# A convolution and a gated unit in one kernel: seven blocks of the unit's last product move behind the planner's last step, and the output of the last Fourier stage leaves two blocks at a time

## The chip, the cores and the metric

The kernel runs on one core of a Trainium2 chip. A core has five engines with instruction queues of their own: TensorE (PE in the profile, with its weight loads as PEld), VectorE (DVE), ScalarE (ACT), GpSimd (POOL) and SyncE (SP). SP, ACT and POOL can each issue DMAs; 16 DMA engines carry them. The metric is the device time of the program in microseconds; a kernel that is timed several times is given by its median.

## The reference

The input `x` has 2048 tokens of 448 channels in float32. It is normalized per token, and the result `xn` goes two ways, whose sum with `x` is the output:

```python
xn = layernorm(x)
dt = exp(log_dt);  A = -exp(log_A_real) + 1j * A_imag;  C = (C_real + 1j * C_imag) * dt
K  = 2 * real(sum_n C[d, n] * exp(A[d, n] * dt[d] * l))       # 448 kernels of 2048 taps, N = 256 modes
y  = irfft(rfft(xn, 4096) * rfft(K, 4096))[:2048] + xn * D_skip   # a causal convolution per channel
g, u = xn @ w_gate, xn @ w_up                                  # 448 -> 1792
out = x + y + (sigmoid(g) * u) @ w_down                        # 1792 -> 448
```

## The kernel before

**Two programs on one core.** `conv()` builds the convolution: it generates the taps, takes their spectra and those of `xn`, multiplies them and transforms back. `glu()` is the gated unit. Both are Python generators that emit instructions and then yield a cost. A small planner at the end of the kernel always advances the generator whose done share (`done[i] / total[i]`) is the smaller. That sets the order in which the two programs' matmuls stand on PE: a matmul group of one is emitted behind the last group of the other (`issue_after`). `total[1]` is the unit's whole cost less `HELD`, so a smaller `total[1]` makes the unit look further on than it is, and lets the convolution go first more often.

**The gated unit.** The 2048 tokens are 16 blocks of 128, in four accumulators `accs[0..3]` of four blocks each ("acc" in the profile). They are worked in two halves of 8 blocks, and the 14 slices of 128 hidden features in groups of at most three. For a slice and four blocks, `gate` runs two groups of 11 matmuls ("gu", L706; float32 values are split into a high and a low part, so a product is three of them), then ACT takes the tanh (`th`), DVE multiplies (`hf`), ACT casts (`hh`, L722) and DVE takes the rest (`hl`, L724). When a group of slices is through, the down product of each block is 9 matmuls for a group of three slices ("po", L818) and one addition to `acc` on DVE (L823). In the last group of the second half (`final`) the two accumulators are `accs[2]` (blocks 8 to 11) and `accs[3]` (blocks 12 to 15); `t` counts these two, and `b` the blocks in one.

**The last stage of the convolution.** `spectra` goes through 17 steps. A step is `there` ("sp", L902: 32 matmuls into four PSUM banks, copies `kc` on ACT L910, and eight products and sums on DVE L913 to L916) and, one step later, `back` ("pv", L929: 16 matmuls, two copies `vt` on ACT L935). `back` and `there` of a round are emitted together, with the loads of the step three rounds ahead. From `vt` four DMAs on SP store to `v_d` (L947), and when they have landed one DMA on SP loads 16 rows of it back as `vp` (L953). When all steps of a half of the channels (`h`; 224 each) are there, `last(h, m)` for m = 0, 2, 4, 6 runs 32 matmuls each (L964) and adds the result to two blocks in each of two accumulators (L972): m = 0 and 2 to blocks 0 to 7 in `ac`, m = 4 and 6 to blocks 8 to 15 in `accs[2]` and `accs[3]`. The banks of `there`, `back` and `last` are four in turn.

**Order at the end.** At (t, b) = (0, 3) of the final group the unit yields `None`: from there on it is held until the convolution has emitted its last instruction, the `vp` load of the last step. Five blocks, (0, 3) to (1, 3), are thus emitted behind the last `back`, beside the path from `vt` over `v_d` to `vp`. Then `last(1, m)` follows, which needs `vp`.

**The output.** `out` writes four blocks of one half of the channels with four DMAs, 32 partitions each (L238), and deals the DMAs in turn to SP, ACT and POOL. The framework gives the DMAs of SP and ACT together eight completion semaphores in turn and those of POOL eight others; a DMA waits at its queue until the one that had its semaphore before has landed. A block's first channel half is complete when its down products and `last(0, m)` are, its second when `last(1, m)` is.

Of the kernel before, what the change touches and what calls it, by code (L numbers as in the profile page):

```python
# [20 lines left out]
D = 448  # L21
# [12 lines left out]
WP = 5  # L34
WX = 2
HELD = 9
HP = 300
Y0 = (8, 1)
CP = D // 4
H = D // 2  # L40
# [89 lines left out]
def s4d_glu_kernel(ctx, tc, io):  # L130
# [5 lines left out]
    x_t, out_t = tok(io["A_u"][0]), tok(io["out"][0])  # L136
# [90 lines left out]
    accs = [acc_tile() for _ in range(2)]  # L227

    def blocks(t, g, b0, nb):
        return t[g, :, b0 // 8, b0 // 4 % 2, b0 % 4 : b0 % 4 + nb]  # L230

    def out(src, b0, h):

        ds = slice(H * h, H * h + H)
        for g in range(4):
            eng = (nc.sync, nc.scalar, nc.gpsimd)[outs[0] % 3]
            outs[0] += 1
            eng.dma_start(blocks(out_t, g, b0, 4)[:, :, ds], src[32 * g : 32 * g + 32, :, ds])  # L238

    def x_load(dst, b0, nb, engs):  # L240
        for g in range(4):
# [211 lines left out]
    def kgen(pk):  # L453
# [15 lines left out]
        nc.gpsimd.memset(pms[0][:, 6], 1.0)  # L469
        with hp(HP):  # L470
            for _ in powers(pms, 0, None):
# [95 lines left out]

        with hp(HP):
            phase_load(0)
# [8 lines left out]
        for g in range(NCK // NCH):  # L578
            for c in range(NCH):
# [49 lines left out]
                if cn % 4 == 2 and cn > 3 or cn + 1 == NCK:  # L629

                    with hp(HP) if cn + 1 == NCK else tc.issue_after(glu_mm[0].ins):
                        first_stage((cn - 3) // 4 if cn + 1 < NCK else cn // 4)
# [94 lines left out]
    def glu():  # L727
        stores, later = [], []
        for half in range(2):
# [4 lines left out]
            for fs_ in ORDER[half]:  # L734
# [3 lines left out]
                final = half == 1 and fs_ is ORDER[1][-1]  # L738
# [67 lines left out]
                for t in range(2):  # L806
                    acc = accs[2 * half + t]
                    for b in range(4):
                        if final and (t, b) == (0, 3):

                            yield None
                        po = psg.tile([128, D], F32, name="po", tag="gu", bufs=4)
                        bs = slice(128 * b, 128 * b + 128)
                        n = 0
                        with tc.issue_after(sp_mm[0].ins) if glu_on else nullcontext():
                            for (hh, hl), (dh, dl) in zip(hs[t], wts):
                                for a_, w_ in ((hh, dh), (hh, dl), (hl, dh)):
                                    glu_mm[:] = [nc.tensor.matmul(  # L818
                                        po, a_[:, bs], w_, start=(n == 0), stop=(n == 3 * fc - 1)
                                    )]  # L820
                                    n += 1
                        with hp(HP):
                            v.scalar_tensor_tensor(  # L823
                                acc[:, b], po, 0.5, acc[:, b], ALU.mult, ALU.add
                            )
                        yield 0.6 * fc
                        if cross and (t, b) in downs:
                            step(*downs[t, b])
                    if cross:
                        nc.sync.dma_start(acc_d[:, 4 * t : 4 * t + 4], acc)  # L830
                    if final:
                        out(acc, 8 + 4 * t, 0)
                if final:
                    sp_mm[:] = glu_mm
                    for m in range(0, 8, 2):
                        lasts[0](1, m)
                    for t in range(2):
                        out(accs[2 + t], 8 + 4 * t, 1)

    def spectra(pf):  # L840

# [113 lines left out]
        def last(h, m):  # L955

            pos = [bank("pv") for _ in range(2)]
            for i in range(2):
                for g in range(4):
                    for b in range(2):  # L960
                        s = slice(64 * b, 64 * b + 64)
                        w = 8 * g + m + i
                        with after():
                            mm = nc.tensor.matmul(  # L964
                                pos[b][32 * g : 32 * g + 32, i], wf[s, w], vp[h][s, w],
                                start=True, stop=True, skip_group_check=True,
                            )
            sp_mm[:] = [mm]
            for b in range(2):
                q, o, ds = 2 * (m // 4) + b, m % 4, slice(H * h, H * h + H)  # L970
                acc = ac[:, 4 * q + o : 4 * q + o + 2, ds] if q < 2 else accs[q][:, o : o + 2, ds]
                v.tensor_tensor(acc, acc, pos[b], ALU.add)  # L972
            if m % 4 == 2 and m < 4:
                for q in range(2):
                    out(ac[:, 4 * q : 4 * q + 4], 4 * q, h)

        ac = acl[0]
# [11 lines left out]
        for n, (h, k) in enumerate(steps):  # L989
# [21 lines left out]
            while len(wait) > 1 and not (due and wait[0][0] == 1):  # L1011
                t = wait.pop(0)
                turned(*t)
                if t == (0, 28):
                    due = [n + 1]
            prev = (h, k, cur)
            glu_on[:] = [1]
            yield WS
        sp_mm[:] = glu_mm
# [94 lines left out]
    lasts, glu_mm, sp_mm, glu_on, outs, x1s, hfs, xls = [], [], [], [], [0], [0], [], []  # L1114
    xq, psc, raws, acl, marks, slots, pqs = list(x_first), [], [], [], [None, None], {}, []
    W1s, GGs, act = [], [], []
    gens = [conv(), glu()]
    total = [sum(Y0) + 11 * WP + 8 * WX + 14 + NCK * WK + HOLE + 17 * WS, 2 * (4 + NFT * 14.8) - HELD]
    done = [0.0, 0.0]
# [40 lines left out]
```

## Time and profile before

| | |
|---|---|
| median of 3 runs | 730.58 us (728.54 to 733.38) |
| profiled execution | 727.83 us, of which the profile's span is 726.1 us |
| PE busy | 677.6 us, 93% of the span |
| DVE busy | 565.7 us, 78% |
| ACT busy | 420.6 us, 58% |
| POOL busy | 384.2 us, 53% |
| DMA | 115.71 MB, mean 159 GB/s |
| granted TensorE clock, mean | 0.98 |

The profile is one execution. Times in its rows are microseconds from the start of the span. A row of the timeline gives start, duration, engine, line, operation, output and inputs, a count of merged instructions and, in brackets, how long the engine had been idle and what ended that. The chain of waits is followed back from the last instruction: each piece was released by the one before it. A "q" behind an engine is its instruction queue, where DMAs are issued.

### The profile page before, as it was taken

Reading aid. Unit: us, or ns where it says so; the run is one execution under the profiler, and the core shown is the slowest. Engines: PE = TensorE matmul, PEld = TensorE weight load, DVE = VectorE, ACT = ScalarE, POOL = GpSimd, SP = SyncE. Lnnn points to the kernel's source line nnn. Section 1 sums busy time; section 2 is a strip of 40 time slices with the busy share of each in tenths; the row PEclk is TensorE's granted clock in tenths of the full one; section 3 lists DMA queues with packets and bytes.
Section 4 is the critical chain, followed back from the end, with each engine's and each line's share of the span. In section 5 each row is a group of like instructions: output and inputs, shape, how many; then the busy total and the mean of one; then the engine's idle time right before and its main releaser. Section 6 shows DMA issues by size and latency. Waiting matters only on the chain.

```text
span 726.1 us, 19068 instructions
## 1 busy us (share of the span) xinstructions
PE 677.6 (93%) x7780; PEld 533.8 (74%) x7780; DVE 565.7 (78%) x776; ACT 420.6 (58%) x650; POOL 384.2 (53%) x423
## 2 busy tenths in 40 slices
PE   2898799899998999998999999999999999999994
PEld 1674688787886888655778887888877787767783
DVE  5699997699999999999499988986956555664553
ACT  3645455578787788898388678767643312323310
POOL 2110018698899988788557856767844002431001
PEclk9998899999999999999999999999999999999998
DMA  9946328525414554454952232232269999999646
GB/s 203 229 108 183 104 80 248 164 93 177 167 51 135 185 158 147 135 162 130 270 183 102 83 108 97 71 108 94 58 172 271 273 235 234 233 244 221 166 131 162
DMA packets 92710, 115.71 MB, mean 159 GB/s; under 512 B 12112, under 2 KB 81104, under 8 KB 92368
## 3 DMA queue, kind: packets, MB, share of 16 engines
q1 hardware_dynamic: 83312, 94.03, 47.2%
q10 hardware_dynamic: 6736, 14.57, 6.4%
q0 software_dynamic: 2576, 5.90, 3.3%
q8 instruction: 61, 1.00, 0.6%
q14 instruction: 25, 0.20, 0.1%
HBM read 69.70 MB, written 44.76 MB: 158 GB/s over the span
## 4 chain that ended last, share of the span: by engine, by line
PE 58%; DVE 17%; POOL 8%; DMA 7%; issue 3%; ACT 3%; SPq 2%; ACTq 0%; POOLq 0%; DVEq 0%
PE gu L706 23%; PE po L818 12%; PE sp L902 7%; PE ko L614 5%; PE pv L929 4%; POOL me L511 4%; PE tr L533 3%; DVE Et L599 2%; DVE Et L598 2%; DVE Ft L600 2%; DVE hl L724 2%; POOL mf L511 2%; DMA acc_d<-acc 1%; DVE wl L761 1%; DVE pm L447 1%
## 5 line engine op out<-in xcount | busy, mean ns | idle before, releaser
L511 POOL TENSOR_TENSOR me<-me,pm 128x32 f32<-128x32 f32 (+1 forms) x168 | 155.9, 928 | 78.1 <-DVE Et L599 65.5
L511 POOL TENSOR_TENSOR mf<-mf,pm 128x64 f32<-128x64 f32 (+1 forms) x112 | 116.5, 1040 | 4.9
L706 PE MATMUL gu<-xh,wh 128*128 128x512 f32 x336 | 101.1, 407 | 2.5 <-ACT xh L219 2.5
L706 PE MATMUL gu<-xh,wl 128*128 128x512 f32 x336 | 95.4, 392 | 0.0
L706 PE MATMUL gu<-xl,wh 128*128 128x512 f32 x336 | 95.1, 390 | 0.0
L818 PE MATMUL po<-dh,hh 128*128 128x448 f32 x224 | 86.8, 387 | 6.0 <-DVE acc L823 2.5
L598 DVE TENSOR_TENSOR Et<-me,S 128x1024 f32<-128x1024 f32 x56 | 81.8, 1460 | 7.2 <-ACT S L544 5.5
L599 DVE TENSOR_TENSOR Et<-me,S 128x1024 f32<-128x1024 f32 x56 | 79.3, 1415 | 7.8 <-ACT me L524 7.7
L818 PE MATMUL po<-dl,hh 128*128 128x448 f32 x224 | 84.5, 377 | 0.0
L541 ACT ACTIVATE S<-tr 128x1024 f32<-128x1024 f32 x56 | 57.8, 1032 | 45.3 <-PE tr L533 40.3
L600 DVE TENSOR_TENSOR Ft<-mf,S 128x1024 f32<-128x1024 f32 x56 | 78.7, 1405 | 6.8 <-ACT S L544 5.0
L818 PE MATMUL po<-dh,hl 128*128 128x448 f32 x224 | 83.7, 375 | 0.0
L706 PEld LDWEIGHTS gu<-xh,wh 128*128 128x128 f32 x336 | 62.3, 193 | 21.3 <-ACT xh L219 4.0
L722 ACT CAST hh<-hf 128x512 fp32r<-128x512 f32 x56 | 35.0, 625 | 70.0 <-DVE hf L717 57.6
L706 PEld LDWEIGHTS gu<-xh,wl 128*128 128x128 f32 x336 | 62.9, 188 | 14.9 <-DVE pl L307 0.7
L706 PEld LDWEIGHTS gu<-xl,wh 128*128 128x128 f32 x336 | 63.0, 188 | 13.9 <-issue 0.7
L614 PEld LDWEIGHTS ko<-Et,Ft 128*32 128x32 f32 x3584 | 53.8, 110 | 25.7 <-issue 14.7
L614 PE MATMUL ko<-Et,Ft 128*32 128x64 f32 x3584 | 63.9, 222 | 7.6 <-DVE Ft L600 4.2
L717 DVE SCALAR_TENSOR_TENSOR hf<-th,gu 128x512 f32<-128x512 f32 x56 | 38.2, 682 | 38.4 <-PE gu L706 28.0
L544 ACT ACTIVATE S<-S,hpi 128x1024 f32<-128x1024 f32 x56 | 65.7, 1173 | 0.0
L823 DVE SCALAR_TENSOR_TENSOR acc<-po,acc 128x448 f32<-128x448 f32 x80 | 48.5, 616 | 21.7 <-PE po L818 21.7
L724 DVE TENSOR_TENSOR hl<-hf,hh 128x512 fp32r<-128x512 f32 x56 | 51.2, 915 | 13.2 <-ACT hh L722 13.2
(196 smaller groups left out, 1286.5 us busy)
## 6 DMA issues: line engine op xcount, KB each, us to landing
sk_d<-sk ACTq DMA_DIRECT2D x14, 512.0 KB
sx<-x_d SPq DMA_DIRECT2D x32, 224.0 KB
skl<-sk_d SPq DMA_DIRECT2D x16, 448.0 KB
vp<-v_d SPq DMA_DIRECT2D x16, 448.0 KB
v_d<-vt SPq DMA_DIRECT2D x62, 112.0 KB
wt_d<-wh SPq DMA_DIRECT2D x9, 512.0 KB
wt_d<-wl SPq DMA_DIRECT2D x9, 512.0 KB
wl<-wt_d SPq DMA_DIRECT2D x9, 512.0 KB
```

The lines of the kernel that those rows point to most:

```text
L511: ins = nc.gpsimd.tensor_tensor(m[:, :, w + a : 2 * w : n], m[:, :, a:w:n], par(base + i).unsqueeze(2).to_broadcast([128, 4 * DC, w // n]) ...
L541: nc.scalar.activation(rows(cs), pv, AF.Abs)
L544: sins[:] = [nc.scalar.activation(cs, cs, AF.Sin, scale=-TWO_PI, bias=hpi)]
L598: v.tensor_tensor(Et[:, :, :, 32:64], two(me[:, :, 32:64]), S[:, 1::-1], ALU.mult)
L599: v.tensor_tensor(Et[:, :, :, 0:32], two(me[:, :, 0:32]), S[:, 1:3, :, ::-1], ALU.mult)
L600: fts[:] = [v.tensor_tensor(Ft, two(mf), S[:, 3:5], ALU.mult)]
L614: nc.tensor.matmul(ko[32 * j : 32 * j + 32, sl], Ft[:, cc, DC * h + 4 * q + j], Et[:, cc, DC * h + 4 * q + j], start=(k == 0), stop=(k == ...
L706: glu_mm[:] = [nc.tensor.matmul(ps, a_, b_, start=(n == 0), stop=(n == len(mm) - 1))]
L724: v.tensor_tensor(hl, hf, hh, ALU.subtract)
L818: glu_mm[:] = [nc.tensor.matmul(po, a_[:, bs], w_, start=(n == 0), stop=(n == 3 * fc - 1))]
L823: v.scalar_tensor_tensor(acc[:, b], po, 0.5, acc[:, b], ALU.mult, ALU.add)
L902: mm = nc.tensor.matmul(to, tb[:kk, t, 64 * c : 64 * c + 64], rhs, start=True, stop=True, skip_group_check=True,)
```

## The change

Four things change.

- The unit is held from (0, 1) on, not from (0, 3): seven blocks are kept for the time behind the last `back`.
- Of these, five ((0, 1) to (1, 1)) are emitted ahead of `last(1, m)` as before, and two ((1, 2) and (1, 3)) behind it. Each of the two leaves at once with both channel halves, by four DMAs. The first halves of blocks 8 to 11 leave behind (0, 3), those of blocks 12 and 13 behind (1, 1).
- `last(1, m)` hands out its two blocks per accumulator at once, where it had waited for four: eight DMAs at m = 0 and at m = 2, four (of `accs[2]`) at m = 4 and at m = 6. The second halves of blocks 12 and 13 follow behind m = 6.
- `LATE = 3.6` is taken from `total[1]` after round 11 of `spectra`, so that the planner's order shifts from there.

```diff
+LATE = 3.6
...
-    def out(src, b0, h):
-
-        ds = slice(H * h, H * h + H)
+    def out(src, b0, h=None):
+
+        ds = slice(0, D) if h is None else slice(H * h, H * h + H)
         for g in range(4):
             eng = (nc.sync, nc.scalar, nc.gpsimd)[outs[0] % 3]
             outs[0] += 1
-            eng.dma_start(blocks(out_t, g, b0, 4)[:, :, ds], src[32 * g : 32 * g + 32, :, ds])
+            eng.dma_start(blocks(out_t, g, b0, src.shape[1])[:, :, ds], src[32 * g : 32 * g + 32, :, ds])
...
-                        if final and (t, b) == (0, 3):
+                        if final and (t, b) == (0, 1):
 
                             yield None
...
+                        if final and t == 1 and b > 1:
+                            out(acc[:, b : b + 1], 12 + b)
+                        if final and (t, b) == (1, 1):
+                            out(acc[:, 0:2], 12, 0)
+                            sp_mm[:] = glu_mm
+                            for m in range(0, 8, 2):
+                                lasts[0](1, m)
+                            out(acc[:, 0:2], 12, 1)
                         yield 0.6 * fc
                         if cross and (t, b) in downs:
                             step(*downs[t, b])
                     if cross:
                         nc.sync.dma_start(acc_d[:, 4 * t : 4 * t + 4], acc)
-                    if final:
-                        out(acc, 8 + 4 * t, 0)
-                if final:
-                    sp_mm[:] = glu_mm
-                    for m in range(0, 8, 2):
-                        lasts[0](1, m)
-                    for t in range(2):
-                        out(accs[2 + t], 8 + 4 * t, 1)
+                    if final and t == 0:
+                        out(acc, 8, 0)
...
-            if m % 4 == 2 and m < 4:
+            if h == 1 and m < 4:
+                for q in range(2):
+                    out(ac[:, 4 * q + m : 4 * q + m + 2], 4 * q + m, h)
+            elif h == 1:
+                out(accs[2][:, m - 4 : m - 2], 4 + m, h)
+            elif m == 2:
                 for q in range(2):
                     out(ac[:, 4 * q : 4 * q + 4], 4 * q, h)
...
             prev = (h, k, cur)
+            if n == 11:
+                total[1] -= LATE
             glu_on[:] = [1]
```

Up to `last(0, 0)` and `last(0, 2)`, the first of the L964 rows below, PE's order is what it was. On PE just behind them, before the change ("gu" is half a `gate`, the five rows from `xh,wh` to `xl,wh`; "pv" with `yy,bk` is `back`):

```order
L964 MATMUL pv<-vp,wf 32x224 x32
L706 MATMUL gu<-xh,wh 128x512 x3
L706 MATMUL gu<-xr,wh 128x512
L706 MATMUL gu<-xh,wl 128x512 x3
L706 MATMUL gu<-xr,wl 128x512
L706 MATMUL gu<-xl,wh 128x512 x3
L706 MATMUL gu<-xh,wh 128x512 x3
L706 MATMUL gu<-xr,wh 128x512
L706 MATMUL gu<-xh,wl 128x512 x3
L706 MATMUL gu<-xr,wl 128x512
L706 MATMUL gu<-xl,wh 128x512 x3
L929 MATMUL pv<-yy,bk 128x224 x8
```

And in the same place with the change, where every line number is one or three higher:

```order
L967 MATMUL pv<-vp,wf 32x224 x32
L707 MATMUL gu<-xh,wh 128x512 x3
L707 MATMUL gu<-xr,wh 128x512
L707 MATMUL gu<-xh,wl 128x512 x3
L707 MATMUL gu<-xr,wl 128x512
L707 MATMUL gu<-xl,wh 128x512 x3
L932 MATMUL pv<-yy,bk 128x224 x8
L905 MATMUL sp<-skl,tb 64x224 x4
L905 MATMUL sp<-sx,tb 64x224 x4
L905 MATMUL sp<-skl,tb 64x224 x4
L905 MATMUL sp<-sx,tb 64x224 x4
L967 MATMUL pv<-vp,wf 32x224 x32
```

Round 12 (`back`, `there` and `last(0, 4)`, `last(0, 6)`) stands half a `gate` earlier, and so it goes on. Counted from these rows, the halves of `gate` that stand ahead of the six remaining `back`s were 2, 4, 5, 7, 7 and 7 and are 1, 2, 4, 5, 7 and 7; of the final group's blocks of "po", one and three stood ahead of the last two `back`s, and now none and one.

At PE's end, before the change (the last block, `last(1, m)`, the end):

```order
L818 MATMUL po<-dh,hh 128x448
L818 MATMUL po<-dl,hh 128x448
L818 MATMUL po<-dh,hl 128x448
L964 MATMUL pv<-vp,wf 32x224 x64
L1156 UNCONDITIONAL_BRANCH
```

And with the change, where the first three rows below `last(1, m)` stand six times, for blocks (1, 2) and (1, 3):

```order
L967 MATMUL pv<-vp,wf 32x224 x64
L819 MATMUL po<-dh,hh 128x448
L819 MATMUL po<-dl,hh 128x448
L819 MATMUL po<-dh,hl 128x448
```

Eighteen matmuls of "po" have gone from ahead of the last stage to behind it. The queue of SP at its end, before the change:

```order
L947 DMA v_d<-vt 32x4x224 x4
L238 DMA out_dram<-acc 32x4x224
L953 DMA vp<-v_d 16x7168
L238 DMA out_dram<-acc 32x4x224 x2
L238 DMA out_dram<-ac 32x4x224 x2
L238 DMA out_dram<-acc 32x4x224 x3
```

And with the change:

```order
L950 DMA v_d<-vt 32x4x224 x4
L956 DMA vp<-v_d 16x7168
L239 DMA out_dram<-acc 32x4x224
L239 DMA out_dram<-acc 32x2x224 x2
L239 DMA out_dram<-ac 32x2x224 x5
L239 DMA out_dram<-acc 32x2x224 x4
L239 DMA out_dram<-acc 32x448 x3
```

The `vp` load stands ahead of the first output DMA, and behind it SP issues 15 outputs in place of 8. In the same stretch ACT issues 14 and POOL 15, each in place of 8.

## The prediction

> **What bounds the kernel now.** First the page, by engines and by slices of 18.2 us:
>
> ```profile
> span 726.1 us, 19068 instructions
> ...
> PE 677.6 (93%) x7780; PEld 533.8 (74%) x7780; DVE 565.7 (78%) x776; ACT 420.6 (58%) x650; POOL 384.2 (53%) x423
> ...
> PE   2898799899998999998999999999999999999994
> ```
>
> PE is the bound, and in the second half almost without a gap. All that the change moves lies in the last four or five slices. So I look there next, at what PE waits for from 640 us on:
>
> ```profile
> PE pv L964 <- DVE pd L914: 1.2, 1, 1.2
> PE pv L964 <- DMA vp<-v_d: 1.0, 1, 1.0
> ```
>
> These are two waits, 2.2 us in all, both ahead of a `last`. The first lies ahead of the place where the order begins to differ and stays as it is. Everything else up to the last `last` is PE's own time: a matmul taken from ahead of it moves the end forward, as long as no chain of waits turns up in its place. The chain of waits over the end, start and duration:
>
> ```profile
> 690.08 2.02 PE po L818 x9
> 692.10 1.71 PE pv L929 x16
> 693.81 3.18 PE sp L902 x32
> 696.99 3.85 PE po L818 x18
> 700.84 1.76 PE pv L929 x16
> ...
> 705.00 2.83 DMA v_d<-vt
> ...
> 707.91 4.82 DMA vp<-v_d
> ```
>
> The last `back` starts at 700.84, behind three blocks. From there the path goes over the memory to `vp`, beside which PE works on five blocks. Behind that, PE's last row, DVE's and the end of the queues:
>
> ```profile
> 712.86 4.30 PE L964 MATMUL pv<-vp,wf 64*32 64x224 f32 x128 [1.00 <-DMA vp<-v_d]
> ...
> 711.89 0.62 DVE L823 SCALAR_TENSOR_TENSOR acc<-po,acc 128x448 f32<-128x448 f32 x1 [1.20 <-PE po L818]
> 713.92 2.21 DVE L972 TENSOR_TENSOR ac<-ac,pv 128x448 f32<-128x448 f32 x4 [1.41 <-PE pv L964]
> 716.06 2.21 DVE L972 TENSOR_TENSOR acc<-acc,pv 128x448 f32<-128x448 f32 x4
> ...
> L1156 POOLq DRAIN  x3: 46/102/6607, 718.6 to 725.7; - x3
> L1156 SPq DRAIN  x3: 7/7/7, 724.6 to 725.4; - x3
> ...
> 717.00:718.00 1.00, 0.15 (x4) 0.00 (x0) 1.00 (x3) 0.00 (x0) 0.54 (x1) 1.00 0.85 242
> 722.00:723.00 1.00, 0.00 (x0) 0.00 (x0) 0.00 (x0) 0.00 (x0) 0.00 (x0) 0.50 1.03 323
> 723.00:724.00 1.00, 0.00 (x0) 0.00 (x0) 0.00 (x0) 0.00 (x0) 0.00 (x0) 0.50 0.35 117
> ```
>
> The last two numbers of a window's row are the busy share of the DMA engines and GB/s. From 717 to 723 us the DMA engines are full, at 242 to 323 GB/s, with the second channel halves of all 16 blocks (1.84 MB; at some 285 GB/s 6.4 us). SP, which waits for every DMA, is through at 724.6. POOL's drain, which begins with its last DMA at 718.6 and is the 6.6 us one of the three, ends at 725.2, 0.6 us later; then come 0.9 us. So the tail behind the start of `last` at 712.86 is 11.7 us to SP and 12.3 us to POOL.
>
> **The change part by part.** I count from 712.86, the start of the last `last`, and then its tail.
>
> *Two blocks leave the path.* The piece at 696.99 is 18 matmuls, 3.85 us. They now stand behind `last`; one block remains ahead of the last `back`. Does the `back` then wait for its inputs? DVE needs until about 2.3 us after the last "sp" for them, and the first `back` matmuls need only the first half of them. At 690.08 one block, 2.02 us, already stood between the two, and "pv" followed at 692.10 with no gap. So: **-3.85 us**.
>
> *The planner's shift.* Round 12 comes half a `gate` earlier: one half (2.7 us) lies between `last(0, 2)` and its `back`, not two. What PE, ACT and DVE did there:
>
> ```profile
> 649.49 5.21 PE gu L706 x22
> 654.70 1.71 PE pv L929 x16
> 656.42 3.18 PE sp L902 x32
> 659.60 2.65 PE pv L964 x64
> ...
> 650.62 3.87 ACTq L238 DMA_DIRECT2D out_dram<-ac  x3
> 654.53 0.62 ACT L722 CAST hh<-hf 128x512 fp32r<-128x512 f32 x1 [8.94 <-DMA out_dram<-ac]
> ...
> 656.45 0.97 ACT L935 COPY vt<-pv 128x448 f32<-128x448 f32 x2 [0.80 <-PE pv L929]
> ...
> 658.20 0.62 DVE L913 TENSOR_TENSOR yy<-kc,sp 128x448 f32<-128x448 f32 x1 [2.33 <-PE sp L902]
> 658.74 0.61 DVE L914 TENSOR_TENSOR pd<-kc,sp 128x448 f32<-128x448 f32 x1
> ```
>
> ACT stands in its three output issues until 654.5, and behind them in its queue are the cast `hh` and then `vt`, whose banks `there` needs. Before, the 5.21 us of "gu" covered that. Now `back` runs from 652.2 to 653.9, `there` would end at 657.1 and `last` follow at once. But `vt` can only be copied after 654.53 + 0.62 = 655.15, and ends at 656.1; the second pair of banks of `there`, wanted at 655.5, comes 0.2 to 0.6 us late. `kc` stands behind `vt`: the first product pair of DVE then runs from 656.65 to 657.75, where `last` wants its bank at 657.3 (0.5 us), and the second half of `last` loses some 0.3 us likewise. I take **+1.1 us**, between 0 (all of it taken up) and 2.2 (each doubled). The DMAs of the round (four stores, four loads, three `vp`) go 1 to 4 us earlier on SP, which stood idle there from 652.6 to 657.0; later rounds have one or two halves of `gate` between "sp" and "pv" as before and cost nothing.
>
> *The gap of the last stage.* It holds five blocks as before, but the outputs of blocks 8 to 11 leave behind the third block of the five, not the first, some 3.6 us later against `back`. How long SP waited between its last store and `vp`, in the last round but one and in the last:
>
> ```profile
> 694.40 3.17 SPq L947 DMA_DIRECT2D v_d<-vt  x4
> 699.12 0.53 SPq L953 DMA_DIRECT2D vp<-v_d  x1
> 703.14 2.46 SPq L947 DMA_DIRECT2D v_d<-vt  x4
> 705.65 0.59 SPq L238 DMA_DIRECT2D out_dram<-acc  x1
> 707.91 0.53 SPq L953 DMA_DIRECT2D vp<-v_d  x1
> ```
>
> 699.12 - 697.57 is 1.55 us; 707.91 - 705.60 is 2.31 us, with the outputs beside the stores. Without them `vp` starts 0.75 us earlier, and its 4.82 us still cover the wait of 1.00 us. I take **-0.7 us**, between -1.0 (the wait is all there is to win) and +0.5 (the outputs now lie beside the landing of `vp`).
>
> Sum: `last` starts at 712.86 - 3.85 + 1.1 - 0.7 = 709.4.
>
> *The tail.* `last` lasts 4.30 us and the two blocks 3.85 us; then the addition of 0.62 us. The last block is ready 8.8 us behind 709.4, and its second DMA on SP is issued some 0.45 us later. Rows of L238, the outputs around 650 us (few others beside them) and the ones from 712 us on (full engines):
>
> ```profile
> DMA to landing us min/median/max: 2.4/2.5/2.6
> ...
> DMA to landing us min/median/max: 3.2/4.4/4.8
> ```
>
> Meanwhile the other 1.6 MB begins to leave with m = 0, 1.7 us behind the start (713.92 + 0.62 against 712.86), 1.1 us sooner than before (half of the 2.21 us). Allowing 1.8 us until the engines are full, with 5.6 us at some 285 GB/s it is through about 9.1 us behind the start. So the last block finds the engines nearly empty and I take 2.5 us: landed at 11.75, against 11.7 before, **0**; between -0.3 and +1.9 (4.4 us).
>
> *POOL's drain.* Its last DMA comes at 8.8 behind `last` now, and came at 5.7 (718.6). What the drain of 6.6 us waits for, one execution doesn't tell. If it is as long whenever it begins, it ends at 709.4 + 8.8 + 6.6 = 724.8 against 725.2: the kernel ends **0.4 us** earlier and nearly all of the win is lost. If it follows the landing of POOL's own DMAs (718.58 + 4.4 = 723.0, and 2.2 us more), it ends at 718.2 + 2.8 + 2.2 = 723.2: **-2.0 us**. If it follows the last landing of all, **-3.4 us**. I take the middle one: POOL's is the queue that the drain stands in.
>
> Sum: 727.83 - 2.0 = 725.8 us in terms of the profiled execution. The median of the runs stands 2.75 us above that execution, so in its terms 730.58 - 2.0 = **728.6 us**. A change of this kernel below 1%, 7.3 us, can't be told from none.
>
> **The rivals.** *The drain has a fixed length.* For it: it begins with the last DMA, and SP was through 0.6 us before it ended. Against: 6.6 us is far more than the other two drains, 0.05 and 0.1 us. 727.4 in the profile's terms, 730.2 by the median.
>
> *The whole win.* The drain ends with the landings: 727.83 - 3.4 = 724.4, by the median 727.2.
>
> *Slower: small output DMAs that wait for each other.* In place of 16 outputs of 115 KB behind `last` there are 28 of 57 KB and eight for the last two blocks. SP and ACT have 24 of these and eight completion semaphores, so three go through each, one after the other. If a DMA of half the size takes as long to land under load (4.4 us), the third lands at 1.7 + 3 x 4.4 = 14.9 us behind `last`, where 11.7 was: +3.2 us; with the upper stall of 2.2 us the sum is -3.85 + 2.2 - 0.7 + 3.2 = **+0.9 us**, 731.5 by the median. It decides once a landing takes more than (11.7 - 1.7) / 3 = 3.3 us. Against it: 4.4 us is the time in full engines, half of the bytes in flight empty sooner, and behind the queued outputs on SP, ACT and POOL stands nothing but outputs. The Trainium skill ("DMA: Bandwidth & Descriptors", section on bandwidth) speaks for this rival: it would have DMAs batched, and counts transfers under 64 KB as bound by their descriptors, with 138 GB/s at 64 KB. By that rate, an estimate, 1.84 MB would take 13.3 us in place of 6.4. The trace disagrees as far as it goes: DMAs of 115 KB, many in flight, ran at up to 323 GB/s, close to what that page has for 1 MB (341). No run shows 57 KB.
>
> **How the numbers follow.** The middle drain 0.40, the fixed one 0.25, the whole win 0.20, the slower rival 0.15. No case reaches 7.3 us on its own; only with the scatter of the runs (728.54 to 733.38) could it: faster by over 1% 0.05, slower 0.07, within 0.88. The range: below, 727.2 and a scatter of 1.8; above, the slower rival's 731.5 with 0.7 on top: 725.4 to 732.2.
>
> **What would show it.** In the profile after: the last L964 starts near 709.4, with a wait for `vp` under 0.5 us; two new short waits of PE at "sp" and L964 near 655 to 661 us; 18 "po" behind L964; the last landing some 11.7 us behind its start; POOL's drain then tells which of the three it is. I am wrong if PE waits more than 2.2 us near round 12, if `vp` lands later against `back` than it did, or if the output queues are still at work 3 us after the last addition has been issued.

## The result and the profile after

The changed kernel took **728.32 us** (median, 725.02 to 736.09) beside 731.47 us of the kernel before on the same chip (728.20 to 738.99): a ratio of **0.9952, 95% interval 0.9930 to 0.9974**, some 3.5 us faster. The ratio leaves out the one run of 736.09 us, which fell into a slower state. The forecast was 728.6 us and "within 1%" (7.3 us). The profiled execution took 725.02 us against 727.83, 2.8 us less. Repeated among other kernels, the changed kernel came to 728.24 beside 730.35, ratio 0.9988 (0.9962 to 1.0013; the two medians alone stand at 0.9971): the gain is small enough that a second set of runs doesn't separate it from none. What speaks for a gain all the same is the whole of the runs below: all nine sets with the two blocks behind `last` came out between 0.9940 and 0.9988, the two without at 0.9999 and 1.0008.

The page of the changed kernel, by engines and PE's slices:

```profile
span 723.2 us, 19101 instructions
...
PE 676.3 (94%) x7780; PEld 532.4 (74%) x7780; DVE 565.1 (78%) x776; ACT 420.8 (58%) x650; POOL 384.5 (53%) x430
...
PE   2998799997998999998999999999999999999996
```

PE does the same 7780 matmuls; its last slice is fuller (6 tenths, 4 before), since the two moved blocks stand in it. The chain that ended last, from behind the last `there` on, start and duration:

```profile
694.67 2.02 PE po L819 x9
696.69 1.71 PE pv L932 x16
698.40 9.49 PE po L819 x45
707.89 1.67 PE pv L967 x64
709.58 2.55 PE pv L967 x64
712.13 2.06 PE po L819 x9
714.21 0.64 DVE acc L824
714.85 0.28 issue
715.13 0.47 POOL out_dram L239
715.63 0.51 POOL out_dram L239
716.14 0.82 issue
716.97 0.52 POOLq L1166
```

One block stands ahead of the last `back`, five behind it, and the chain goes straight from the five to `last`: the step over the memory (`v_d`, `vp`), which was on it before, is gone. Behind `last` come two blocks, and then not DVE or a landing but POOL's queue. PE's row in the timeline, with no releaser in brackets behind the last `last`, and the two waits near the first one:

```profile
647.63 0.96 PE L967 MATMUL pv<-vp,wf 64*32 64x224 f32 x16 [0.41 <-DVE pd L917]
...
658.27 0.96 PE L967 MATMUL pv<-vp,wf 64*32 64x224 f32 x16 [0.40 <-DVE pd L917]
...
707.82 4.30 PE L967 MATMUL pv<-vp,wf 64*32 64x224 f32 x128
```

The last `last` starts at **707.82** (712.86 before, 709.4 forecast). What follows it took 15.41 us to the end of the span; before, 13.20. So of 5.04 us won up to there, 2.2 were lost behind it. The queue rows of the end (kind, number, and durations in ns: least, median, most), to be read beside those of the kernel before in the prediction:

```profile
L1166 POOLq DRAIN  x3: 46/93/5495, 717.0 to 723.0; - x3
L1166 SPq DRAIN  x3: 7/7/7, 721.0 to 722.7; - x3
```

POOL's drain begins at 717.0 and takes 5.5 us, to 722.5; SP was through at 721.0. Before, it took 6.6 us, from 718.6 to 725.2, with SP through at 724.6.

### The profile page after: what moved, and what is told of

It is laid out like the page before. It is cut to its first block, busy times and chain, and to the rows that moved or that the text cites. A ratio compares the mean times of both kernels' runs of the same rounds, so it can differ in the third digit from the quotient of the medians.

```text
span 723.2 us, 19101 instructions
## 1 busy us (share of the span) xinstructions
PE 676.3 (94%) x7780; PEld 532.4 (74%) x7780; DVE 565.1 (78%) x776; ACT 420.8 (58%) x650; POOL 384.5 (53%) x430
## 4 chain that ended last, share of the span: by engine, by line
PE 62%; DVE 16%; ACT 8%; DMA 7%; issue 4%; SPq 2%; POOL 1%; ACTq 0%; DVEq 0%; POOLq 0%
PE gu L707 24%; PE po L819 15%; PE sp L905 7%; PE ko L615 6%; PE pv L932 4%; PE tr L534 3%; DVE Et L600 2%; DVE Ft L601 2%; DVE Et L599 2%; DVE hl L725 1%; DMA acc_d<-acc 1%; DVE pm L448 1%; ACT S L545 1%; DMA xe<-in_A_u_dram 1%; DVE wl L762 1%
## 5 line engine op out<-in xcount | busy, mean ns | idle before, releaser
L512 POOL TENSOR_TENSOR me<-me,pm 128x32 f32<-128x32 f32 (+1 forms) x168 | 146.1, 870 | 83.5 <-DVE Et L600 70.8
L512 POOL TENSOR_TENSOR mf<-mf,pm 128x64 f32<-128x64 f32 (+1 forms) x112 | 120.7, 1078 | 4.9
L615 PE MATMUL ko<-Et,Ft 128*32 128x64 f32 x3584 | 65.5, 225 | 8.1 <-DVE Et L599 4.6
L725 DVE TENSOR_TENSOR hl<-hf,hh 128x512 fp32r<-128x512 f32 x56 | 51.8, 925 | 12.5 <-ACT hh L723 12.5
```

The lines of the kernel that those rows point to most:

```text
L512: ins = nc.gpsimd.tensor_tensor(m[:, :, w + a : 2 * w : n], m[:, :, a:w:n], par(base + i).unsqueeze(2).to_broadcast([128, 4 * DC, w // n]) ...
L615: nc.tensor.matmul(ko[32 * j : 32 * j + 32, sl], Ft[:, cc, DC * h + 4 * q + j], Et[:, cc, DC * h + 4 * q + j], start=(k == 0), stop=(k == ...
L725: v.tensor_tensor(hl, hf, hh, ALU.subtract)
```

## The experiments

To compare executions I cut each profile at two points: the start of the first `last(0, 0)` and that of the last stage's `last(1, 0)`, called L from here on. "First" is the time by which PE is late at the first `last` (over its undisturbed 2.65 us) and by which the `gate` behind it is slow; "round 12" is what `there` and `last` of that round take over 3.18 and 2.65 us; "to L" goes from the first point to the second, "end" from L to the end of the span, "drain" is when POOL's drain ends behind L. All in us, from one profile each; before and after are the first two rows. The ratio is that to the kernel before, with its 95% interval.

| kernel | first | round 12 | to L | drain | end | ratio |
|---|---|---|---|---|---|---|
| before | 1.12 | 0 | 67.20 | 12.31 | 13.20 | 1 |
| after | 0.36 | 0.36 | 62.31 | 14.64 | 15.41 | 0.9952 (0.9930 to 0.9974) |
| the shift alone | 0 | 2.31 | 67.86 | 12.16 | 13.04 | 0.9999 (0.9966 to 1.0031) |
| without the shift | 0 | 1.38 | 64.07 | 14.56 | 15.34 | 0.9983 (0.9952 to 1.0013) |
| outputs by four | 4.81 | 0 | 66.59 | 14.30 | 15.08 | 0.9983 (0.9951 to 1.0014) |
| last two blocks not on POOL | 2.67 | 0 | 64.35 | 11.51 | 13.59 | 0.9955 (0.9920 to 0.9991) |
| both of these | 5.36 | 0 | 67.06 | 11.67 | 13.33 | 0.9960 (0.9931 to 0.9989) |
| no late output on POOL | 0 | 0 | 61.61 | 6.70 | 15.04 | 0.9972 (0.9945 to 1.0000) |
| outputs by two alone | 2.94 | 0 | 68.81 | 12.89 | 13.67 | 1.0008 (0.9969 to 1.0048) |
| after, again | 0.76 | 1.72 | 64.17 | 14.57 | 15.35 | 0.9988 (0.9962 to 1.0013) |
| no late output on POOL, drain late | 0 | 0 | 61.59 | 13.45 | 15.09 | (one execution) |
| `wh`, `wl` in pieces | 0.81 | 1.42 | 63.81 | 14.58 | 15.36 | 0.9966 (0.9933 to 0.9998) |
| by four, last two not on POOL, in pieces | 0 | 1.02 | 62.67 | 11.83 | 13.48 | **0.9940 (0.9914 to 0.9967)** |

The columns add up. In all nine profiles that have the whole order of the changed kernel, "to L" less "first" and "round 12" is 61.6 to 61.8. Of the kernel before (67.20 - 1.12) it is 66.1, and in the other profile with that order, "outputs by two alone", 65.9. So the change of order is worth **some 4.4 us** (4.1 to 4.5 by the choice of profiles), and the two columns ahead are what an execution adds to it, up to 5.4 us. That is why medians, not single spans, are compared, and why a tail is read from L on.

**The shift alone.** The kernel before with the planner's table alone; no block moves behind `last`:

```diff
+LATE = 3.6
+            if n == 11:
+                total[1] -= LATE
```

> The planner's shift alone (LATE in the kernel before; the unit is held from (0, 3), outputs as before). The order then has one block ahead of the last back and seven beside the path to vp. My account: PE's work ahead of the last stage is as before; the seven blocks cover the wait for vp (1.0 us goes), a stall of some 0.4 us comes at round 12 as in the changed kernel. The last stage starts 0.3 to 1.0 us earlier than before and the span ends as much earlier: 725.1 to 725.8 us against 726.1. Rival, that the shift is what won the time and not the two blocks: the last stage starts 3 to 5 us earlier and the span is near 723.

It took 730.49 us beside 731.22: no difference. Its waits of PE, summed, number and longest:

```profile
PE sp L903 <- ACT vt L936: 1.4, 1, 1.4
PE pv L965 <- DVE pd L915: 0.7, 1, 0.7
```

Seven blocks then lie behind the last `back`, and the wait for `vp` of 1.00 us is gone, but round 12 pays 2.1 us in waits, where 0.4 had been expected. Without that, "to L" is 65.6 us, 0.5 less than before and within what was expected; with it, the shift by itself wins nothing.

**Without the shift.** The changed kernel with `LATE = 0.0`:

> The changed kernel with LATE = 0. The last there is then followed directly by the last back, with no block between. My account: PE waits for DVE's products there, 1.5 to 2.3 us, the 0.4 us stall at round 12 goes; the last stage starts 1 to 2 us later than in the changed kernel (at 709 to 710 us) and the span is 724.3 to 725.2. Rival, that the shift does nothing: 723.2 as in the changed kernel and no wait of PE at that back above 0.5 us.

It took 729.80 us beside 731.22. Its waits of PE:

```profile
PE pv L932 <- DVE yy L918: 0.9, 2, 0.7
PE sp L905 <- ACT vt L938: 0.7, 1, 0.7
PE pv L967 <- DVE pd L917: 0.6, 1, 0.6
```

The last `back` stands directly behind the last `there` and waits 0.9 us for `yy` (1.5 to 2.3 expected), which the one block ahead of it hides in the changed kernel. That is the worth of the shift for the two moved blocks. And round 12 stalls here too, against what was expected, so the stall isn't the shift's alone. ACT's rows there, of this kernel and of the second profile of the changed one:

```profile
654.49 4.22 ACTq L239 DMA_DIRECT2D out_dram<-ac  x3
658.75 0.62 ACT L723 CAST hh<-hf 128x512 fp32r<-128x512 f32 x1 [10.44 <-DMA out_dram<-ac]
...
659.76 0.95 ACT L938 COPY vt<-pv 128x448 f32<-128x448 f32 x2
```

```profile
653.13 3.76 ACTq L239 DMA_DIRECT2D out_dram<-ac  x3
656.94 0.62 ACT L723 CAST hh<-hf 128x512 fp32r<-128x512 f32 x1 [9.53 <-DMA out_dram<-ac]
657.46 0.96 ACT L938 COPY vt<-pv 128x448 f32<-128x448 f32 x2
```

The three output issues hold ACT's queue for about 4 us, and `hh` and `vt` come straight behind. What PE made of that in the second profile:

```profile
656.12 0.93 PE L905 MATMUL sp<-sx,tb 128*64 128x224 f32 x8
658.04 0.98 PE L905 MATMUL sp<-skl,tb 128*64 128x224 f32 x8 [0.99 <-ACT vt L938]
...
661.98 0.96 PE L967 MATMUL pv<-vp,wf 64*32 64x224 f32 x16 [0.56 <-DVE pd L917]
```

How late the round is follows from one time. In all ten profiles with the shift, what round 12 pays is, to within 0.1 us, how far the end of ACT's third output issue trails the start of `back`, less 1.6 us, and nothing below that: 1.93 us behind and 0.36 paid in the changed kernel, 3.30 and 1.72 in its second profile, 1.52 and 0 in "no late output on POOL, drain late". Each time this third issue left within 0.04 us of the landing of the DMA that had its semaphore before. This is read from the profiles; no run set that time by itself.

**Outputs by four.** The changed kernel, but behind `last(1, m)` blocks 0 to 11 leave by four blocks (12 DMAs of 115 KB), not by two (24 of 57 KB):

```diff
-            if h == 1 and m < 4:
-                for q in range(2):
-                    out(ac[:, 4 * q + m : 4 * q + m + 2], 4 * q + m, h)
-            elif h == 1:
-                out(accs[2][:, m - 4 : m - 2], 4 + m, h)
-            elif m == 2:
+            if m == 2:
                 for q in range(2):
                     out(ac[:, 4 * q : 4 * q + 4], 4 * q, h)
+            elif h == 1 and m == 6:
+                out(accs[2][:, 0:4], 8, h)
```

> The changed kernel, but the second halves of blocks 0 to 11 leave by four blocks again (eight DMAs behind m = 2 and four behind m = 6, not eight, eight, four and four). Theory that the eight semaphores of SP and ACT hold back the last block's DMAs: with 12 DMAs less, the last block's four are issued within 1.0 us of its addition (they took until 2.4 us behind it), the last landing is 11.4 to 12.0 us behind the start of the last stage in place of 12.8, and the span is 0.5 to 1.3 us shorter, 722 to 722.7. Rival, that the early start of the output pays more: the engines are still full when the last block comes, the last landing is 12.8 us or more behind, and the span is 723.2 to 724.5.

The last output was issued at L + 10.1 in place of 11.25, so the small DMAs did wait for each other; but it landed at 12.5 in place of 12.8, and POOL's drain still ended last: the end moved by 0.3 us, to L + 15.1. The landing was expected at 11.4 to 12.0 by the one account and at 12.8 or later by the other, so it bears out neither.

**The last two blocks not on POOL.** The changed kernel, its two whole blocks dealt to SP and ACT alone:

```diff
-            eng = (nc.sync, nc.scalar, nc.gpsimd)[outs[0] % 3]
+            eng = (nc.sync, nc.scalar)[outs[0] % 2] if h is None else (nc.sync, nc.scalar, nc.gpsimd)[outs[0] % 3]
```

> The changed kernel, but blocks 14 and 15 leave by SP and ACT alone, so that POOL's last DMA is issued near 714 us and not 717. What does POOL's drain wait for? If it lasts 5.5 to 6.6 us from POOL's last DMA, or ends 2.2 to 2.8 us behind the landing of POOL's own DMAs, it ends near 720.5, ahead of SP, and SP's drain (721 to 722) sets the end: span 722.3 to 723.0. If it waits for the last landing of all queues (+1.8 us as in the changed kernel), it still ends last, near 722.5 to 723.5, and the span is 723.2 to 724.2.

The queue rows of its end:

```profile
L1166 POOLq DRAIN  x3: 46/93/5372, 717.8 to 725.0; - x3
L1166 SPq DRAIN  x3: 7/7/7, 724.4 to 724.7; - x3
```

POOL's drain ran from 717.8 to 723.1, SP was through at 724.4: POOL no longer sets the end. Against L (711.63) the end comes at 13.6 in place of 15.4, 1.8 us sooner. The medians don't show that gain: the ratio is 0.9955 beside 0.9952. The drain ended 1.1 us ahead of the last landing of all (L + 12.6), so it doesn't wait for that.

**Both.** Outputs by four, and the last two blocks on SP and ACT:

> Outputs behind `last` by four blocks (12 DMAs of 115 KB over the three engines), and the last two blocks on SP and ACT alone. Theory: two things sit one behind the other in the tail of the changed kernel, POOL's drain (2.2 to 2.8 us behind the landing of POOL's own last DMA) and, right under it, output DMAs of SP and ACT that wait for a completion semaphore. With both eased POOL's last DMA goes out near +6.2 us behind the start of the last `last`, lands near +8.9, its drain ends near +11.5; the last output is issued near +10.0 (not +11.25) and lands near +12.1; the kernel ends near +12.9 instead of +15.4, 2.5 us sooner than the changed kernel, a median ratio to the kernel before of about 0.992. Rival: the landing is set by the bytes in the engines, not by the semaphores; then it lands at +12.6 as with the last two blocks off POOL alone, and ends at +13.6.

The end is at L + 13.3, 2.1 us sooner than in the changed kernel. It lies between the two accounts (12.9 with the semaphores, 13.6 with the bytes in the engines), so how much of the landing is due to which stays open. The median, 727.75 beside 730.35, shows little of it: this profile, and perhaps other executions too, lost 5.4 us at the first `last`, on which below.

**No late output on POOL.** Outputs by two as in the changed kernel, but all that come behind the start of `last(1, 0)` on SP and ACT (`if h != 0` in the line above):

> Outputs by two blocks as in the changed kernel, but all 36 output DMAs behind the start of the last `last` on SP and ACT, none on POOL. Theory (semaphores): those two engines share eight completion semaphores, so 4 to 5 DMAs go through each in turn in place of 3; POOL's drain is off the path, but the last output is issued 1.5 to 2.5 us later than the +11.25 of the changed kernel, lands near +15 and the kernel ends near +15.5, no sooner than the changed kernel. Rival (the drain alone sets the end, the wait for semaphores is harmless): the last landing stays at +12.6 and the end is at +13.6, 1.8 us sooner than the changed kernel.

The last output was issued at L + 12.4 (11.25 in the changed kernel), landed at 14.1, and the end is at 15.0: with all late outputs on two queues hardly anything is won, though the last issue came 1.1 us later and not 1.5 to 2.5. SP's rows of the outputs:

```profile
709.92 5.26 SPq L239 DMA_DIRECT2D out_dram<-ac  x8
715.40 4.92 SPq L239 DMA_DIRECT2D out_dram<-acc  x10
```

The issues themselves, counting one long one of 1.9 us, fill 8.4 of these 10.4 us; ACT's fill 8.4 of 11.1. Between them lie 2.0 and 2.7 us, less than the 3.3 and 4.5 us that lie between twelve issues each in the changed kernel, and a landing took 1.9 us at the median where it had taken 2.7. So this run doesn't show that the wait for completion semaphores grows with the number of DMAs: here it is mostly the number of issues on two queues. POOL's queue row:

```profile
L1166 POOLq DRAIN  x3: 46/93/5707, 709.2 to 723.0; - x3
```

The drain took its 5.7 us here as well, far from the end and for nothing.

**The drain by itself.** The same kernel with one cast on POOL behind the last addition, whose result nothing uses. POOL's DMAs have all landed then:

```diff
+                        if final and (t, b) == (1, 3):
+                            nc.gpsimd.tensor_copy(d_low(), acc[:, b])
```

> The kernel with all late output DMAs on SP and ACT, and one cast of 0.6 us on POOL behind the last addition (its result is used nowhere), so that POOL's drain begins near +9.6 behind the start of the last `last`, some 5 us after POOL's own last DMA has landed (near +4.7). If the drain follows the landings of POOL's own DMAs alone, nothing is left to wait for: it ends less than 1 us after it began, near +10.5, and SP sets the end near +15.0. If it has a floor of its own of 5.2 to 5.7 us, as the lengths of ten profiles (5.2 to 6.6) would also allow, it ends near +15.0 and the kernel near +15.8. If it waits for the last landing of all (near +14), it ends near +14.5 to +16.

The timeline row of the cast, and the queue row:

```profile
716.85 0.56 POOL L830 CAST dl<-acc 128x448 fp32r<-128x448 f32 x1 [7.31 <-DVE acc L824]
```

```profile
L1168 POOLq DRAIN  x3: 46/102/4593, 716.8 to 722.8; - x3
```

POOL's last DMA had landed at 712.8, 4 us earlier, and still the drain took 4.6 us (4.0 behind the end of the cast). So waiting for its own landings can't be all that the drain does: a part of 4 to 4.6 us is its own. None of the three ends expected (near +10.5, +15.0, +14.5 to 16) is the one measured, +13.45, and it is one execution; whether a drain behind a cast is as long as one behind nothing at all no run shows. Waiting for every landing is excluded again (it ended 0.7 us ahead of the last one).

**Outputs by two alone.** The kernel before, with only the outputs behind `last(1, m)` by two blocks:

```diff
-            if m % 4 == 2 and m < 4:
+            if h == 1:
+                for q in range(2) if m < 4 else (2, 3):
+                    src = ac[:, 4 * q + m : 4 * q + m + 2] if q < 2 else accs[q][:, m - 4 : m - 2]
+                    out(src, 4 * q + m % 4, h)
+            elif m == 2:
                 for q in range(2):
                     out(ac[:, 4 * q : 4 * q + 4], 4 * q, h)
```

> The kernel before with one part of the change alone: behind `last(1, m)` the outputs leave by two blocks, no block of the gated unit is moved. Theory: the first bytes leave 1.1 us sooner, the last addition still ends at +5.4 behind the start of the last `last`, and the DMAs of half the size wait through the semaphores; the two cancel within 0.7 us, landing +10.8 to +11.8, POOL's own last landing +9.5 to +10.5, end +12.5 to +13.6 (before: +13.2); ratio 1.000 within 0.003. Rival (the slower rival of the prediction): three DMAs go one after the other through a semaphore, the last one lands at +14.9, the kernel is 3 us slower, ratio 1.004. Other rival: outputs by two are a gain of their own of 1 us or more, end below +12.2.

Landing at L + 11.1 (11.5 before), end at 13.7 (13.2, and 13.6 at most expected): the two effects of smaller DMAs cancel, a little on the wrong side, because POOL issues 11 of them at 0.54 us each behind L where it had issued 5, so that its drain begins 1.5 us later and ends 0.6 us later. Ratio 1.0008. This part of the change is worth nothing by itself.

**The changed kernel again.**

> The changed kernel itself, beside the others on the same chip. Theory: its end lies 15.4 us behind the start of the last `last`, of which POOL's drain ends 2.2 to 2.8 us behind the landing of POOL's own last DMA; the wait of PE in round 12 is between 0 and 1.3 us, with the wait at the first `last` ahead of it; a ratio of 0.995 within 0.003. Rival: the first measurement was a lucky one and the ratio is 1.000.

Tail and drain are as in its first profile (15.35 and 14.57 behind L), round 12 stalled 1.7 us (1.3 at most expected), and the ratio was 0.9988, just outside the 0.992 to 0.998 expected. Its interval and the first one overlap (0.9962 to 0.9974), so the first may have been on the lucky side; 1.000 isn't excluded by this set alone.

**POOL's `wh` and `wl` in pieces.** The profile of "both" lost most at the first `last`. DVE's and POOL's rows around it:

```profile
645.83 0.61 DVE L917 TENSOR_TENSOR pd<-kc,sp 128x448 f32<-128x448 f32 x1
646.36 1.16 DVE L918 TENSOR_TENSOR yy<-yy 128x224 f32<-128x224 f32 x1
647.55 2.42 DVE L919 TENSOR_TENSOR yy<-pd 128x224 f32<-128x224 f32 x1
```

```profile
646.23 1.04 POOL L769 CAST wh<-wraw 128x1024 fp32r<-128x1024 f32 x1 [5.63 <-DMA wraw<-in_B_w_up_dram]
647.36 2.37 POOL L770 TENSOR_TENSOR wl<-wraw,wh 128x1024 fp32r<-128x1024 f32 x1
```

A `yy` takes 0.38 to 0.39 us alone. Here the first lasts until POOL's cast ends (647.3), the second until `wl` ends (649.7). `pd` is late by that, and PE waited for it:

```profile
PE pv L967 <- DVE pd L917: 2.8, 1, 2.8
```

Products with one operand in PSUM (`sp`) aren't held. POOL's and DVE's rows of the changed kernel in its first profile:

```profile
643.39 2.36 POOL L770 TENSOR_TENSOR wl<-wraw,wh 128x1024 fp32r<-128x1024 f32 x1
```

```profile
644.18 0.62 DVE L916 TENSOR_TENSOR yy<-kc,sp 128x448 f32<-128x448 f32 x1 [3.94 <-PE sp L905]
644.72 0.61 DVE L917 TENSOR_TENSOR pd<-kc,sp 128x448 f32<-128x448 f32 x1
645.25 0.75 DVE L918 TENSOR_TENSOR yy<-yy 128x224 f32<-128x224 f32 x1
```

Two of them run for their 0.61 us inside `wl`, and only the `yy` behind them lasts until `wl` is through (645.75, and 0.25 more). The Trainium skill ("SBUF — State Buffer", section "Who interferes with whom") states this as a lock: a VectorE operation with two SBUF inputs and a GpSimd operation that reads SBUF block each other for a whole instruction. These rows agree: each held `yy` ends 0.25 us behind the POOL operation. When `wl` runs depends, by the rows of nine of the eleven profiles with whole operations, on the landing of `wraw`; it started between 641.9 and 653.6 us, and in ten of the eleven it or the cast held a `yy` near the first `last`, by 0.4 to 2.0 us, the kernel before among them (one `yy` of 1.50 us). So the last rounds' `wh` and `wl` in four pieces each, in the changed kernel and in "both":

```diff
-                            nc.gpsimd.tensor_copy(wh, raw)
-                            nc.gpsimd.tensor_tensor(wl, raw, wh, ALU.subtract)
+                            for i in range(2):
+                                for k in (slice(0, 2), slice(2, 4)):
+                                    nc.gpsimd.tensor_copy(wh[:, i, k], raw[:, i, k])
+                                    nc.gpsimd.tensor_tensor(wl[:, i, k], raw[:, i, k], wh[:, i, k], ALU.subtract)
```

> The changed kernel, with POOL's cast `wh` and subtraction `wl` of the last rounds in four pieces of 256 columns in place of one of 1024. Theory: DVE's `yy` operations with both inputs in SBUF wait until a POOL operation that runs beside them has ended (they took up to 2.42 us in place of 0.39 beside `wl` of 2.37 us); beside pieces of about 0.6 us they take at most 1.0 us, the wait of PE at the first `last` falls to 0.7 us or less (0.4 to 3.6 in the profiles so far), the granted clock behind it stays at 1.00, and from the start of the first `last` to that of the last one it takes 61.6 to 63.0 us. The median falls by 1 to 2 us against the changed kernel: ratio to the kernel before 0.994. Rival: DVE doesn't get in between the pieces; an operation of DVE still ends with the last piece, rows of 1.2 us and more stay, the wait of PE goes up to 3.6 us as before, and the ratio is that of the changed kernel, 0.995 to 0.999.

> All three edits that the runs point to in one: outputs behind `last` by four blocks, the last two blocks not on POOL, `wh` and `wl` of POOL in four pieces. Theory: the tail ends at +13.3 as with the first two edits alone, the wait of PE at the first `last` is 0.7 us or less; 3 to 4 us sooner than the changed kernel, ratio to the kernel before 0.991. Rival: the pieces of POOL gain nothing; ratio 0.996 as without them.

In the first of these two the pieces met the same operations:

```profile
646.22 2.94 POOL L772 TENSOR_TENSOR wl<-wraw,wh 128x256 fp32r<-128x256 f32 x4
```

```profile
647.79 0.78 DVE L920 TENSOR_TENSOR yy<-yy 128x224 f32<-128x224 f32 x1
648.60 0.81 DVE L921 TENSOR_TENSOR yy<-pd 128x224 f32<-128x224 f32 x1
```

0.78 and 0.81 us beside four pieces of 0.7 us, where whole operations had held them for 1.2 to 2.4: DVE does get in between. PE waited 0.9 us at the first `last` (0.7 expected at most), with the clock at 1.00. By the median, 727.62 beside 730.21, it can't be told from the changed kernel: this execution had 1.4 us of round 12 besides. In the profile of the second no `yy` ran beside the pieces at all, so its undisturbed first `last` doesn't speak for them. All three edits together took **726.02 us** beside 730.21, ratio 0.9940: 4.2 us faster than before, with the end at L + 13.5; 0.991 had been expected. Its interval overlaps that of the changed kernel (0.9930 to 0.9974), so that it beats that one is likely by its tail and not shown by the medians.

## Why the prediction was right

The median forecast, 728.6, was met to 0.3 us, and the sum in terms of the profiled execution (725.8) to 0.8. Part of the first is luck: the forecast was 2.0 us off a median of 730.58 from three runs, and among the runs of the comparison the kernel before stands at 731.47, so a gain of 2.0 was forecast and one of some 3.5 measured. The mechanism held in the main; two terms missed in opposite directions. By the steps:

- **Two blocks leave the path, -3.85.** Right; the 18 "po" now stand behind `last`, and the last `back` found its inputs ready behind one block. The run without the shift shows what the block hides: 0.9 us.
- **The planner's shift, +1.1 (0 to 2.2).** The mechanism was right, in place and chain: ACT's output issues, `hh`, `vt`, then `there`, then `last`. In the first profile only the second of the two waits shows, in the next both. Of the size, one execution had 0.36, the next 1.72; over the ten profiles with the shift it was 0 to 2.31, 0.7 in the mean. It isn't the price of the shift alone, since the kernel without it paid 1.38 in its one profile. Not foreseen: the round is late or not by when ACT's third output finds its semaphore, and that differs from execution to execution (by the relation above the prediction's own times, 654.5 and 652.2, give 0.7). The halved `gate`s also cost PE 0.23 us, two pieces of 2.72 where one of 5.21 stood, which the sum left out.
- **The gap of the last stage, -0.7 (-1.0 to +0.5).** The whole wait of 1.00 us went. The load of `vp` left 0.7 us earlier against the last `back`, as forecast, and landed 0.3 us before `last` began; in all, `last` came 0.9 us earlier against `back`. With so little to spare, a further block moved away would, as an estimate, bring the wait back.
- **The last `last` at 709.4.** 707.82, of which 0.75 is not the change's: the wait at the first `last`, ahead of the changed order, fell from 1.16 to 0.41 us by chance, as it would have for the kernel before.
- **The tail, 0 (-0.3 to +1.9).** This term failed in size: the last landing came 12.83 us behind L, where 11.75 was forecast. The last addition was ready when forecast (8.87 against 8.8). But the step "its second DMA on SP is issued some 0.45 us later" did not hold. SP's and ACT's rows, start and whole stretch of the outputs:

```profile
713.88 4.84 SPq L239 DMA_DIRECT2D out_dram<-acc  x7
```

```profile
714.76 4.64 ACTq L239 DMA_DIRECT2D out_dram<-acc  x6
```

  Seven issues of at most 0.45 us are spread over 4.84 us on SP, six over 4.64 on ACT; between them each queue waits for the landing of the DMA that had the semaphore before. The last left ACT at 719.07, 2.4 us behind the last addition. That is the mechanism of the slower rival, at two fifths of its size (+1.3 us on the last landing, not +3.2): on SP and ACT a landing took 1.6 to 3.7 us, 2.7 at the median, where the rival needed more than 3.3. By the prediction's own third sign, output queues at work 3 us after the last addition has been issued, this step fails narrowly: the addition was issued at 716.07, and ACT was at work until 719.40. ACT's last landing took 1.6 us (719.07 to 720.65); the least, median and most of POOL's in the tail:

```profile
DMA to landing us min/median/max: 2.4/2.7/3.6
```

  Small DMAs landed sooner than the 4.4 us of POOL's large ones, while the engines moved up to 277 GB/s, twice the 138 GB/s that the Trainium skill ("DMA: Bandwidth & Descriptors", section "Bandwidth") has at 64 KB in its table, weighed in that rival:

```profile
716.00:718.00 2.00, 0.03 (x1) 0.00 (x0) 0.62 (x1) 0.00 (x0) 0.64 (x2) 1.00 0.89 277
```

- **POOL's drain, -2.0 in sum.** Forecast: the drain ends 2.2 us behind the landing of POOL's own last DMA. It ended 2.7 behind it in the changed kernel, 2.0 to 3.0 in all profiles where a DMA of POOL stood right ahead of it, so the number came out. The reading behind it was only half right. The three rivals, by the runs: a fixed 6.6 us is wrong (4.6 to 6.7); the last landing of all is wrong (in five kernels the drain ended before it); and its own landings alone are wrong too, since 4.6 us remained when nothing of POOL's was in flight. What fits all profiles is a length of its own of 4 to 5.7 us, and up to 6.7 where the last DMA of POOL landed late, 4.2 to 4.4 us behind its issue; in the four profiles with such a landing it ended 2.2 us behind it, in the others with a DMA right ahead 4.7 to 5.1 us behind the end of POOL's last issue. Whether the two run beside each other stays open.

So 1.6 us more than forecast came up to L (0.75 by chance, 0.7 of a stall that was milder in that execution), and 0.8 us were lost behind it (14.64 in place of 13.8): the near hit owes something to both. Without the chance parts, the change is worth 4.4 us up to L less 2.2 behind it, **some 2.2 us** in a profile.

## What to carry to other kernels

Work moved behind the last dependent stage wins its own time on the path only if the end of the kernel moves with it: here 4.4 us became 2.2, because an output behind the last addition went to POOL, whose drain goes on for some 5 us behind it (1.8 of the 2.2 us), and others behind it waited for semaphores already in use. Give the very last outputs to the queues that finish at once, but not all of the late ones: with all of them on two queues the end came at L + 15.0, with only the last two blocks taken off POOL at 13.6. Fewer and larger outputs brought 0.3 us more. When single profiles of one kernel differ by several us, cut them at common points and add up the pieces: the pieces are stable, and the ones that are not have a cause of their own.

## What the hardware showed beside that

- POOL's drain at the end of a program took 4.6 us with nothing in flight and 5.2 to 6.7 right behind a DMA; SP's took 7 ns and ACT's at most 0.16 us. In this kernel the last DMA of POOL should so be issued some 5 to 6 us before the end.
- A wait of PE of 1.1 to 2.8 us at the first `last` was followed in four of the profiles by a lower granted clock. The stretch behind the wait of 2.8 us in the kernel "both" (length, busy time of PE, PEld, DVE, ACT, POOL, then the granted clock, DMA share, GB/s):

```profile
650.00:660.00 10.00, 8.82 (x53) 6.20 (x55) 5.15 (x10) 1.45 (x3) 3.33 (x5) 0.66 0.85 214
```

  There a half of `gate` took 4.5 us in place of 2.7. The kernel before had a wait of 1.16 us at the same place without it, and waits elsewhere, of 1.4 us in "the shift alone" and 1.2 us in "no late output on POOL", had the clock at 1.00 behind them; the others of the four had waits of 1.1 (clock 0.83), 1.4 (0.83) and 1.8 us (0.66). In these four the column "first" is 1.9 to 2.6 times the wait itself; what decides between 1.00 and less wasn't tried.
